# Four attention layers on one core: layer B's state folded into its output weights, PSUM banks handed out singly, loads reordered

## The chip, the cores and the metric

One core of one Trainium2 chip. The metric is the device time of one execution in microseconds; the median of three runs before the change is 563.27 us (559.5 to 564.46).

## The reference

Activations x are 2048 rows of 512 in bf16, 32 heads of 16. Four layers A, B, A, B are each added to x after a layer norm:

```
A: q,k,v = ln(x) @ wqkv;  p = softmax(q k^T / 4) over the keys 0 to 255 rows back;  x + (p v) @ wo
B: pq, pk = phi(q), phi(k)      with phi(t) = (t + 1 if t > 0 else exp(t)) + 1e-6
   kv[h] = sum over rows of pk v^T (16 x 16),   z[h] = sum over rows of pk
   o = (pq kv) / (pq z + 1e-6);   x + o @ wo
```

Both A layers share one set of weights, and both B layers another.

## The kernel before, in words

All of x stays in SBUF in f32 (`xres`, 16 tiles of 128 rows). A superblock I is four tiles, 512 rows; there are four of them. The program is a list of operations, each with a cost per engine, a priority and its dependences; `Planner.run` (L150) is a list scheduler in Python that writes the order of every engine's instructions at build time. At each step it takes the operation that can start first by its own costs, and between equal starts the one with the lower priority number, then the one made first. Operations marked `EV` (priority -1: evacuations) win ties. On the chip the order per engine is fixed and only semaphores decide when an instruction starts.

PSUM has eight banks: a tile of three for one kind of score block (ring "3"), a tile of two for the other (ring "2"), and three single banks (ring "M") for all else: projections, transposes, the p v sums, layer B's products. `Ring.free_at` hands out the buffer that has been free longest.

Layer A, per superblock: `ln_tile` (L399) takes statistics on VectorE, the power on GpSimd and applies them on either; the normalized tile is transposed, by TensorE (`by_pe`) with an evacuation, or by a DMA on SyncE's queue. `prep` (L780) projects k, q and v; k goes into a doubled, masked `kbd` (VectorE, L473), v through `vst` and four DMAs into block-diagonal `vbd` (L492), which is zeroed at the start by GpSimd (L351). `scores` (L497) is matmul, exp on ScalarE (L534) and triangle masks on GpSimd or VectorE; `pv_group` (L571) sums p v and divides; `out_A` (L621) transposes and projects with `woA`.

Layer B, first half (`b_proj`, L787): k and v of four tiles, `phi` (L651: exp on ScalarE, two VectorE operations), the sum into `kvs` (L710), and phi(q) transposed into `pqT` for all 2048 rows. Its work for superblock I is planned between the attention work of later superblocks. When all four are in, `kv_final` (L719) masks the sums into block-diagonal `kvn` and `kvz`. Second half: `den_unit` (L729) multiplies `pqT` by `kvz` for a superblock (16 small matmuls) and takes the reciprocal on VectorE; `p2_tile` (L748) per tile multiplies `pqT` by `kvn` (4 matmuls of 128 columns), multiplies by the reciprocal on VectorE into `ob`, transposes `ob` by TensorE or DMA into `oT`, multiplies by `woB` (4 matmuls of 512 columns), and adds to x, or in the last layer writes `ost` and stores it. For the first B layer these operations are made in the loop of the second A layer, superblock by superblock; for the second they are the last stage.

Loads: x tiles 0 to 3 alternate between SyncE's and ScalarE's queues, wA follows in three pieces on both; woA, wB, woB are three large transfers on SyncE; the other twelve x tiles come by fours on both queues at planned times.

Of the kernel before, what the change touches and what calls it, by code (L numbers as in the profile page):

```python
# [16 lines left out]
P = 128  # L17
# [79 lines left out]
class Ring:  # L97

    def __init__(self, n):
        self.n, self.tiles = n, [None] * n  # L100

    def free_at(self):

        b = [(0.0 if t is None else t.end + .1, k) for k, t in enumerate(self.tiles) if t is None or not t.left]
        return min(b, default=None)


class Slot:
# [13 lines left out]
class Planner:  # L122
# [27 lines left out]
    def run(self, log=None):  # L150
# [9 lines left out]
        ready = {o: max([o.after]) for o in self.ops if not waits[o]}  # L160
# [9 lines left out]
        while ready:  # L170
            best = None
            for o, t in ready.items():
                ok = True
                for s in o.takes:
                    f = s.ring.free_at()
                    if f is None:
                        ok = False
                        break
                    t = max(t, f[0])
                if not ok:  # L180
                    continue
# [10 lines left out]
            for p, t in ready.items():  # L192
                if p is o or e not in p.cost or (p.prio, p.n) >= (o.prio, o.n) or t > start + .02:
                    continue
                if any((s.ring.free_at() or (1e9,))[0] > start + .02 for s in p.takes):
                    continue
# [3 lines left out]
            if e == "PE":  # L200
                if o.kind == "scores" and mode != "scores" or o.kind != "scores" and mode == "scores":
                    start += .05
# [8 lines left out]
            for s in o.takes:  # L211
                s.k = s.ring.free_at()[1]
                s.before = s.ring.tiles[s.k]
                s.ring.tiles[s.k] = s
# [4 lines left out]
            if log is not None:  # L219
                log.append((start, o.end, e, o.kind, o.n, o.prio))  # L220
# [10 lines left out]
def build(ctx, tc, A_x, A_wqkv, A_wo, B_x, B_wqkv, B_wo, out, force_safe=False):  # L231
# [21 lines left out]
    def load_wA():  # L253
        for j in range(3):
            (nc.sync if j % 2 == 0 else nc.scalar).dma_start(
                wA[:, :, j * D:(j + 1) * D], A_wqkv[:, j * D:(j + 1) * D].rearrange("(c p) n -> p c n", p=P))

    def load_rest():
        nc.sync.dma_start(woA[:], A_wo.rearrange("(c p) n -> p c n", p=P))
        nc.sync.dma_start(wB[:], B_wqkv.rearrange("(c p) n -> p c n", p=P))  # L260
        nc.sync.dma_start(woB[:], B_wo.rearrange("(c p) n -> p c n", p=P))

    def load_x(I):
        for u in range(4):
            i = 4 * I + u
            (nc.sync if i % 2 == 0 else nc.scalar).dma_start(x0(i), x_dram[i])

    load_x(0)
    load_wA()

# [13 lines left out]
    nc.vector.tensor_scalar(eo[:, 0:1], eo[:, 1:2], -1.0, 1.0, op0=ALU.mult, op1=ALU.add)  # L284
    ones_bf = consts.tile([P, 1], BF, name="ones_bf")
# [18 lines left out]
    def fast_network(ctx_f):  # L304
        pool = lambda name, bufs, **kw: ctx_f.enter_context(tc.tile_pool(name=name, bufs=bufs, **kw))
        ps3 = pool("ps3", 1, space=PSUM)
        ps2 = pool("ps2", 1, space=PSUM)
        psM = pool("psM", 3, space=PSUM)
# [6 lines left out]
        rings = {"M": Ring(3), "3": Ring(1), "2": Ring(1), "xnT": Ring(3), "xn": Ring(4), "oT": Ring(4), "ost": Ring(3),  # L315
                 "phi": Ring(2), "pks": Ring(3), "vs": Ring(3), "ln": Ring(8), "rden": Ring(2)}
        for k_, r_ in rings.items():
            r_.name = k_
        slot = lambda r: Slot(rings[r])

# [10 lines left out]
        rall = fp.tile([P, NSS, 4, H], F32, name="rall")  # L331
# [3 lines left out]
        kvz = fp.tile([P, NCT, 8], BF, name="kvz")  # L335
# [14 lines left out]
        for k in range(NH):  # L350
            nc.gpsimd.memset(vbd[k][:], 0.0)  # L351
# [10 lines left out]
        def proj(lhs, rhs, prio, reads=(), deps=(), use=(), take=(), pre=None, frees=()):  # L362

            deps = list(deps) + [d for b in frees for d in b.r + b.w]
            s = slot("M")
            t = {}
            def fn(e):
                if pre:
                    pre()
                t["t"] = psM.tile([P, 512], F32, name="ps", tag=f"M{s.k}", bufs=1)  # L370
# [5 lines left out]
        def transpose(src, dst, prio, by_pe, deps, writes=(), use=(), actb=ACTB, take=(), pre=None):  # L376
# [691 lines left out]
```

## Time and profile before

| | us |
|---|---|
| median of three runs | 563.27 |
| the profiled execution's own time | 561.27 |
| its span, first to last instruction | 559.5 |
| TensorE busy | 467.1 (83%) |
| VectorE busy | 385.8 (69%) |
| ScalarE busy | 348.7 (62%) |
| GpSimd busy | 281.4 (50%) |

Busy time is an average over stages. The stages by time: head to 18.5 us, first layer A with the first half of layer B woven in to about 236 us, the end of that first half to 258.5, its second half and the start of the second A layer, that layer to 486, the end of B's first half to 512.7, and B's second half to the end. The granted clock has two levels, 1.2 and 2.4 GHz; a mean between them says how a stretch was shared.

### The profile page before, as it was taken

How to read it: one execution, taken by the hardware profiler on the slowest of the kernel's cores; microseconds unless marked ns; L12 is line 12 of the kernel's file. 1: busy time of each engine (PE TensorE's matmuls, PEld its weight loads, DVE VectorE, ACT ScalarE, POOL GpSimd, SP SyncE). 2: the span in 40 equal slices, each digit the busy share in tenths (PEclk: the TensorE clock that was granted, in tenths of full speed). 3: DMA queues.
4: the chain of work that ended last, by engine and by line, in shares of the span. 5: the costliest groups of instructions: out<-in, count | busy, mean ns of one | idle time of the engine just before them, and what ended most of it. 6: DMA issues, size and time to landing. Idle time of an engine off the chain costs nothing.

```text
span 559.5 us, 14879 instructions
## 1 busy us (share of the span) xinstructions
PE 467.1 (83%) x5828; PEld 240.0 (43%) x5906; DVE 385.8 (69%) x912; ACT 348.7 (62%) x365; POOL 281.4 (50%) x871
## 2 busy tenths in 40 slices
PE   0858979699799999777887979699999999887774
PEld 0324534355445545533433545345555455444332
DVE  2756667477477887657984668687776785969565
ACT  0364838598689999532344759588989899353000
POOL 9343645585385484340752538767767675320000
PEclk9987968899899999798999979999999999998778
DMA  8321313210210120000001023511312120000232
GB/s 274 120 71 47 74 34 69 50 30 21 60 31 12 41 37 2 2 2 1 0 1 41 19 63 61 90 38 27 57 42 40 40 40 2 1 0 3 76 81 75
DMA packets 63789, 24.90 MB, mean 45 GB/s; under 512 B 48352, under 2 KB 63200, under 8 KB 63712
## 3 DMA queue, kind: packets, MB, share of 16 engines
q1 hardware_dynamic: 62032, 22.30, 17.4%
q10 hardware_dynamic: 1680, 1.57, 1.0%
q8 instruction: 48, 0.79, 0.6%
q14 instruction: 29, 0.24, 0.2%
HBM read 6.29 MB, written 2.10 MB: 15 GB/s over the span
## 4 chain that ended last, share of the span: by engine, by line
PE 64%; DVE 14%; DMA 5%; POOL 5%; issue 4%; ACT 3%; SPq 3%; DVEq 0%; ACTq 0%; POOLq 0%
PE ps L372 36%; PE A L516 13%; PE O L587 12%; SPq L492 3%; DMA oT<-ob 3%; ACT pt L534 2%; DVE pqT L660 2%; POOL vbd L351 2%; DVE ln_st L412 2%; DVE xres L454 1%; PE pT L391 1%; DVE rden L744 1%; DVE ob L760 1%; PE pkv L703 1%; DMA vbd<-vst 1%
## 5 line engine op out<-in xcount | busy, mean ns | idle before, releaser
L534 ACT ACTIVATE pt<-A 128x1536 bf16<-128x1536 f32 (+2 forms) x246 | 286.1, 1214 | 71.4 <-PE A L516 39.2
L561 POOL TENSOR_SCALAR_AFFINE_SELECT pt<-pt 128x192 bf16<-128x192 bf16 (+2 forms) x600 | 175.3, 325 | 131.6 <-ACT pt L534 128.6
L516 PE MATMUL A<-qT,kbd 32*128 32x320 bf16 (+4 forms) x1440 | 104.6, 262 | 4.8 <-ACT pt L534 4.4
L587 PE MATMUL O<-vbd,pt 128*128 128x34 bf16 x2880 | 94.8, 180 | 11.1 <-DMA vbd<-vst 10.1
L587 PEld LDWEIGHTS <-pt 128*128 128x128 bf16 x2880 | 83.6, 97 | 35.2 <-issue 19.2
L372 PE MATMUL ps<-xnT,wA 128*128 128x512 bf16 x235 | 68.5, 406 | 14.4 <-ACT pt L534 4.3
L516 PEld LDWEIGHTS <-kbd 32*128 32x128 bf16 x1440 | 38.1, 94 | 78.0 <-issue 71.3
L372 PE MATMUL ps<-wB,xnT 128*128 128x512 bf16 x237 | 63.1, 380 | 2.4 <-DVE o_sb L602 0.4
L556 DVE TENSOR_TENSOR pt<-pt,tri 128x64 bf16<-128x64 bf16 (+4 forms) x217 | 52.3, 267 | 16.2 <-ACT pt L534 15.6
L473 DVE TENSOR_TENSOR kbd<-ps,eo 128x512 bf16<-128x512 f32 x64 | 41.3, 684 | 22.9 <-PE ps L372 20.8
L656 ACT ACTIVATE phi_e<-ps 128x512 bf16<-128x512 f32 x64 | 38.3, 598 | 24.2 <-PE ps L372 22.2
L372 PEld LDWEIGHTS <-xnT 128*128 128x128 bf16 x384 | 31.7, 98 | 40.5 <-issue 11.7
L412 DVE BATCH_NORM_STATS2 ln_st<-xres 128x6 f32<-128x512 f32 (+1 forms) x64 | 43.9, 685 | 7.4 <-DMA xres<-in_A_x_dram 6.9
L416 POOL TENSOR_SCALAR ln_rs<-ln_mv 128x1 f32<-128x1 f32 x64 | 14.5, 227 | 63.6 <-DVE ln_mv L413 61.4
L372 PE MATMUL ps<-woB,oT 128*128 128x512 bf16 x117 | 39.5, 473 | 7.6 <-DMA oT<-ob 4.6
L394 ACT COPY oT<-pT 128x512 bf16<-128x512 bf16 x16 | 9.2, 587 | 58.6 <-PE pT L391 58.6
L372 PEld LDWEIGHTS <-oT 128*128 128x128 bf16 x256 | 24.1, 108 | 45.4 <-issue 18.8
L454 DVE TENSOR_TENSOR xres<-ps,xres 128x512 f32<-128x512 f32 x48 | 32.6, 682 | 13.6 <-PE ps L372 12.7
L372 PEld LDWEIGHTS <-wA 128*128 128x128 bf16 x256 | 22.2, 102 | 42.6 <-issue 24.2
L417 POOL TENSOR_TENSOR ln_rs<-ln_rs,mhalf 128x1 f32<-128x1 f32 x64 | 36.7, 574 | 5.2
L372 PE MATMUL ps<-woA,oT 128*128 128x512 bf16 x118 | 32.4, 393 | 4.5 <-DVE o_sb L602 2.9
L427 POOL TENSOR_SCALAR xn<-xres,ln_mv,ln_rs 128x512 bf16<-128x512 f32 x41 | 32.3, 787 | 5.3 <-DMA oT<-ob 1.1
(72 smaller groups left out, 450.9 us busy)
## 6 DMA issues: line engine op xcount, KB each, us to landing
vbd<-vst SPq DMA_DIRECT2D x128, 34.0 KB, 1.9
out_dram<-ost SPq DMA_DIRECT2D x16, 128.0 KB, 1.7
wB<-in_B_wqkv_dram SPq DMA_DIRECT2D x1, 1536.0 KB, 12.3
xres<-in_A_x_dram SPq DMA_DIRECT2D x8, 128.0 KB, 3.4
xres<-in_A_x_dram ACTq DMA_DIRECT2D x8, 128.0 KB, 2.3
wA<-in_A_wqkv_dram SPq DMA_DIRECT2D x2, 512.0 KB, 9.2
xnT<-xn SPq DMA_TRANSPOSE x44, 2.4
wA<-in_A_wqkv_dram ACTq DMA_DIRECT2D x1, 512.0 KB, 8.6
```

Of the source, the lines that this page charges most:

```text
L372: nc.tensor.matmul(t["t"][:], lhsT=lhs(c), rhs=rhs(c), start=(c == 0), stop=(c == NCT - 1))
L412: nc.vector.bn_stats(t["st"][:], x())
L417: nc.gpsimd.tensor_tensor(t["rs"][:], t["rs"][:], mhalf[:, 0:1], op=ALU.pow)
L427: nc.gpsimd.tensor_scalar(t["xn"][:], x(), t["mv"][:, 2:3], t["rs"][:], op0=ALU.add, op1=ALU.mult)
L454: nc.vector.tensor_tensor(xres[:, i, :], ps()[:], x0(i) if first else xres[:, i, :], op=ALU.add)
L473: nc.vector.tensor_tensor(kbd[r][:, t, :, :, :].rearrange("p m k h -> p (m k) h"), ps()[:, hf * 256:(hf + 1) * 256].unsqueeze(2).to_broadc ...
L516: nc.tensor.matmul(A[:, x, at[x]:at[x] + w, :], lhsT=kbd[half(m)][32 * rg:32 * rg + 32, tt, m % 4, :, :], rhs=qT[I % 2][32 * rg:32 * rg + ...
L534: nc.scalar.activation(body[:, x:y, 0:pos[x], :], t["A"][:, x:y, 0:pos[x], :], ACT.Exp, scale=0.25)
L556: nc.vector.tensor_tensor(v, v, mt, op=ALU.mult)
L561: nc.gpsimd.affine_select(out=v, in_=v, compare_op=ALU.is_ge, fill=0.0, base=1 if kind == 0 else -2, pattern=[[0, n], [2 * sg, 64]], chann ...
L587: nc.tensor.matmul(t["O"][:, u, g, :, :], lhsT=PT[:, s0:s0 + 2, :], rhs=vbd[half(m)][:, m % 4, :, grp[g], :], start=(n == 0), stop=(n == l ...
L656: nc.scalar.activation(t["e"][:], ps()[:], ACT.Exp)
```

## The change

The sums `kvn` are transposed on TensorE and multiplied by `woB` once per layer into `wkv`, so a tile of the second half is four matmuls `pqT` x `wkv` straight into x; `ob`, its transposes and `oT` are gone there. The division moves ahead of it: `norm_unit` broadcasts the denominator over 128 partitions with a masked `zb` (one matmul of 512 columns), takes ln(d + 1e-6) and exp(-...) on ScalarE in place in PSUM, and multiplies `pqT` in place on VectorE. A table set with ln and exp is loaded at the start. All eight PSUM banks are one tensor; `bank()` gives banks 0 to 2 and 3 to 4 to scores and 5 to 7 to the rest, and with `wide` set also 4 and 3. Free buffers go by lowest place, no longer by age. The second VectorE step of phi is split, its first part may go to GpSimd; in some stages k's evacuation may go to ScalarE; `vbd` is zeroed by VectorE. wA comes as k, q, v on SyncE with x 0 to 3 on ScalarE; later x tiles and the other weights come one by one, 128 KB each, on SyncE. Some of the planner's costs change (scores .33 to .23, the four v transfers .4 to 2.45, masks and norms a little up), the check of the softmax sums is made per superblock, and the rings oT and ost have 3 and 2 buffers for 4 and 3.

```diff
-        b = [(0.0 if t is None else t.end + .1, k) for k, t in enumerate(self.tiles) if t is None or not t.left]
+        b = [(max(now, 0.0 if t is None else t.end + .1), k) for k, t in enumerate(self.tiles) if t is None or not t.left]
...
+        def bank(size=1):
+            return Slot(rings["ps"], size, {3: (0,), 2: (3,), 1: (5, 6, 7, 4, 3) if wide[0] else (5, 6, 7)}[size])
...
-    load_x(0)
-    load_wA()
+    for j in (1, 0, 2):
+        nc.sync.dma_start(wA[:, :, j * D:(j + 1) * D], A_wqkv[:, j * D:(j + 1) * D].rearrange("(c p) n -> p c n", p=P))
+    for i in range(4):
+        nc.scalar.dma_start(x0(i), x_dram[i])
+    nc.scalar.preload_act_table_set("natural_log_exp_and_others")
...
-            nc.gpsimd.memset(vbd[k][:], 0.0)
+            nc.vector.memset(vbd[k][:], 0.0)
...
-            pl.op({"SP": .4}, fd, prio, reads=[B("vst", n)], writes=[B("v", half(m0), (m0 % 4) // 2)])
+            pl.op({"SP": 2.45}, fd, prio, reads=[B("vst", n)], writes=[B("v", half(m0), (m0 % 4) // 2)])
...
-                nc.vector.tensor_scalar(t["e"][:], t["e"][:], 1.0, 1e-6, op0=ALU.min, op1=ALU.add)
+                (nc.vector if e == "DVE" else nc.gpsimd).tensor_scalar(t["e"][:], t["e"][:], 1.0, 1e-6, op0=ALU.min, op1=ALU.add)
+            y = pl.op({"DVE": .32, "POOL": (.8, .3)}, f2, EV, deps=[x], use=[es])
...
         def kv_final(prio):
...
+                    nc.vector.tensor_tensor(zb[:, 2 * jj:2 * jj + 2, :], bd[:].unsqueeze(1).to_broadcast([P, 2, P]),
+                                            kvs[jj][:, :, P:P + 1].to_broadcast([P, 2, P]), op=ALU.mult)
...
+            transpose(lambda: kvn[:].rearrange("p t c -> p (t c)"), lambda: kvn[:], prio, True,
+                      [d for jj in range(2) for d in B("kvn", jj).w], writes=[B("kvn", 0), B("kvn", 1)], actb=0.0)
+            for c in range(NCT):
...
+                    nc.tensor.matmul(t["t"][:], lhsT=kvn[:, c, :], rhs=woB[:, c, :], start=True, stop=True)
...
+                evac(lambda c=c: wkv[:, c, :], lambda t=t: t["t"][:], prio, s, deps=[o], writes=[B("wkv", c)], actb=0.0)
...
+        def norm_unit(I, c, prio):
+            s = bank()
             t = {}
+            cols = pqT[:, c, I * 512:(I + 1) * 512]
...
+                nc.tensor.matmul(t["p"][:], lhsT=zb[:, c, :], rhs=cols, start=True, stop=True)
+            o = pl.op({"PE": .22}, f, prio, reads=[B("zb", c // 2), B("pq", I, c)], take=[s], kind="den")
+            def f_r(e):
+                nc.scalar.activation(t["p"][:], t["p"][:], ACT.Ln, bias=eps6[:])
+                nc.scalar.activation(t["p"][:], t["p"][:], ACT.Exp, scale=-1.0)
+            r = pl.op({"ACT": 1.25}, f_r, prio, deps=[o], use=[s])
+            def f_m(e):
+                nc.vector.tensor_tensor(cols, cols, t["p"][:], op=ALU.mult)
+            pl.op({"DVE": .69}, f_m, EV, deps=[r], writes=[B("pq", I, c)], use=[s])
+
+        def p2_tile(i, prio, final=False):
+            out_rows(i, lambda c: pqT[:, c, i * P:(i + 1) * P], lambda c: wkv[:, c, :], prio, [],
+                     reads=[B("pq", i // 4, c) for c in range(NCT)] + [B("wkv", c) for c in range(NCT)], final=final)
...
-        for I in range(1, NI):
-            pl.op({"SP": .2}, lambda e, I=I: load_x(I), 5, writes=b_x[4 * I:4 * I + 4], after=14.0 + 20 * (I - 1))
-        pl.op({"SP": .3}, lambda e: load_rest(), 5, writes=[B("wB"), B("woA"), B("woB")], after=14.0)
+        for i in range(4, NT):
+            pl.op({"SP": .6}, lambda e, i=i: nc.sync.dma_start(x0(i), x_dram[i]), 5, writes=[b_x[i]],
+                  after=(6.0, 24.0, 44.0)[i // 4 - 1] + .7 * (i % 4))
...
+        for c in range(NCT):
+            load(woA, A_wo, B("woA"), c, 16 + 2 * c)
+            for j in range(3):
+                load(wB, B_wqkv, B("wB"), c, 30 + 2 * (4 * j + c), j * D, (j + 1) * D)
+            load(woB, B_wo, B("woB"), c, 70 + 2 * c)
...
         for I in range(NI):
-            R = den_unit(I, 2)
-            for u in range(4):
-                p2_tile(4 * I + u, R, 2, by_pe=True if u % 2 == 0 else False, final=True, actb=0.0)
+            for c in range(NCT):
+                norm_unit(I, c, 2)
+        for i in range(NT):
+            p2_tile(i, 2, final=True)
```

## Rows read from the trace of the kernel before

**Rows 1.** The page: span, engines, granted clock, then the chain of waits by engine.
```profile
span 559.5 us, 14879 instructions
PE 467.1 (83%) x5828; PEld 240.0 (43%) x5906; DVE 385.8 (69%) x912; ACT 348.7 (62%) x365; POOL 281.4 (50%) x871
...
PE 64%; DVE 14%; DMA 5%; POOL 5%; issue 4%; ACT 3%; SPq 3%; DVEq 0%; ACTq 0%; POOLq 0%
```

**Rows 2.** Busy time by stretch, each engine with its instructions; then granted clock, DMA.
```profile
0.00:18.50 18.50, 2.23 (x17) 1.44 (x18) 5.85 (x21) 2.46 (x3) 16.71 (x37) 1.00 0.81 270
36.30:44.70 8.40, 0.48 (x11) 0.36 (x11) 1.13 (x3) 0.64 (x1) 1.53 (x6) 0.67 0.40 99
70.50:74.00 3.50, 0.08 (x4) 0.10 (x1) 1.58 (x4) 0.92 (x1) 0.76 (x3) 0.90 0.05 15
236.00:258.50 22.50, 15.49 (x94) 7.39 (x93) 15.44 (x37) 8.89 (x15) 7.43 (x20) 1.00 0.00 1
258.50:281.70 23.20, 17.93 (x148) 9.75 (x151) 20.15 (x41) 5.21 (x9) 11.50 (x26) 0.85 0.00 1
326.90:363.00 36.10, 27.78 (x395) 14.57 (x399) 24.15 (x59) 23.81 (x22) 24.21 (x75) 0.92 0.39 73
486.00:512.70 26.70, 22.82 (x122) 10.55 (x122) 21.91 (x51) 14.06 (x24) 6.76 (x19) 1.00 0.00 1
512.70:559.50 46.80, 31.33 (x218) 15.59 (x221) 27.82 (x50) 2.34 (x4) 0.00 (x0) 0.76 0.27 70
```

**Rows 3.** Timeline of the head: start, duration, engine, line, operation, idle before.
```profile
3.77 7.47 POOL L351 MEMSET vbd<- 128x2176 bf16 x4
...
13.74 0.23 POOL L416 TENSOR_SCALAR ln_rs<-ln_mv 128x1 f32<-128x1 f32 x1
...
18.50 1.91 PE L372 MATMUL ps<-wA,xnT 128*128 128x512 bf16 x4
```

**Rows 4.** Instructions grouped by line: count, busy us, mean ns, idle before.
```profile
L412 DVE BATCH_NORM_STATS2 ln_st<-xres 128x6 f32<-128x512 f32 (+1 forms) x64 | 43.9, 685 | 7.4 <-DMA xres<-in_A_x_dram 6.9
L349 DVE MEMSET vst<- 128x32 bf16 x2 | 0.2, 85 | 0.1
L286 DVE MEMSET ones_bf<- 128x1 bf16 x1 | 0.1, 59 | 0.0
L394 ACT ACT_TABLE_LOAD x1 | 1.3, 1283 | 2.2 <-issue 2.2
```

**Rows 5.** Timeline of SyncE's queue, the early stretch.
```profile
40.59 5.24 SPq L492 DMA_DIRECT2D vbd<-vst  x8
...
68.33 1.06 SPq L266 DMA_DIRECT2D xres<-in_A_x_dram  x2
```

**Rows 6.** Instructions grouped by line: layer B's second half, and the exponential.
```profile
L756 PE MATMUL pn<-kvn,pqT 128*128 128x128 bf16 x128 | 11.9, 229 | 1.9 <-ACT vst L359 0.8 <-DVE ost L449 0.5 <-DVE ob L760 0.4
L391 PE MATMUL pT<-identb,ob 128*128 128x128 bf16 x64 | 7.8, 259 | 8.6 <-DVE ob L760 8.5
L760 DVE TENSOR_TENSOR ob<-pn,rden 128x512 bf16<-128x512 f32 x32 | 20.6, 684 | 1.8 <-PE pn L756 0.8 <-DVE rden L744 0.2 <-DVE vint L1019 0.2
L744 DVE RECIPROCAL rden<-rden 128x128 f32<-128x128 f32 x8 | 7.6, 953 | 0.2
L656 ACT ACTIVATE phi_e<-ps 128x512 bf16<-128x512 f32 x64 | 38.3, 598 | 24.2 <-PE ps L372 22.2 <-DVE pqT L660 0.8 <-DVE pt L556 0.5
```

**Rows 7.** Timeline from the end of the first layer B.
```profile
258.70 0.49 PE L738 MATMUL pd<-kvz,pqT 128*128 128x8 bf16 x14 [1.31 <-DVE kvz L722]
...
281.69 1.03 PE L372 MATMUL ps<-xnT,wA 128*128 128x512 bf16 x4
```

**Rows 8.** Timeline of the last stage.
```profile
530.39 2.76 PE L372 MATMUL ps<-woB,oT 128*128 128x512 bf16 x12 [0.56 <-DMA oT<-ob]
...
540.12 4.81 PE L372 MATMUL ps<-woB,oT 128*128 128x512 bf16 x12 [0.99 <-DMA oT<-ob]
...
554.29 0.69 DVE L449 TENSOR_TENSOR ost<-ps,xres 128x512 bf16<-128x512 f32 x1 [0.17 <-PE ps L372]
```

More of the change, by code (lines that the diff above doesn't have):

```diff
@@ L159, in run @@
                 users.setdefault(d, []).append(o)
-        ready = {o: max([o.after]) for o in self.ops if not waits[o]}
+        ready = {o: o.after for o in self.ops if not waits[o]}
         mac, warm, mode = {}, {}, ""
@@ L194, in run @@
                     continue
-                if any((s.ring.free_at() or (1e9,))[0] > start + .02 for s in p.takes):
+                if any((s.ring.free_at(s, t) or (1e9,))[0] > start + .02 for s in p.takes):
                     continue
@@ L211, in run @@
             for s in o.takes:
-                s.k = s.ring.free_at()[1]
-                s.before = s.ring.tiles[s.k]
-                s.ring.tiles[s.k] = s
+                s.ring.put(s, s.ring.free_at(s, start)[1])
             for s in o.slots:
@@ L284, in build @@
     nc.vector.tensor_scalar(eo[:, 0:1], eo[:, 1:2], -1.0, 1.0, op0=ALU.mult, op1=ALU.add)
+    eps6 = consts.tile([P, 1], F32, name="eps6")
+    nc.vector.memset(eps6[:], 1e-6)
     ones_bf = consts.tile([P, 1], BF, name="ones_bf")
@@ L330, in fast_network @@
         o_sb = fp.tile([P, 4, D], BF, name="o_sb")
-        rall = fp.tile([P, NSS, 4, H], F32, name="rall")
+        rall = [fp.tile([P, 4, H], F32, name=f"rall{k}") for k in range(2)]
+        okw = fp.tile([P, NSS, 2], F32, name="okw")
+        okt = fp.tile([P, 4 * H], BF, name="okt")
         pqT = fp.tile([P, NCT, S], BF, name="pqT")
@@ L413, in f_bn @@
                 nc.vector.bn_aggr(t["mv"][:, 0:2], t["st"][:])
-            bn = pl.op({"DVE": .85}, f_bn, prio, reads=[B("x", i)], take=[ls])
+            bn = pl.op({"DVE": .9}, f_bn, prio, reads=[B("x", i)], take=[ls])
             def f_rs(e):
@@ L498, in scores @@
             nu = len(units)
-            s = slot(str(size))
+            s = bank(size)
             n = npt[size] % NPT
@@ L523, in scores @@
             reads |= {B("k", half(8 * I + x[0]), p // 4) for (b, p), r in zip(units, runs) for x in r}
[L524 removed]
+            mm = pl.op({"PE": .23}, f_mm, prio, reads=reads, deps=lastmm + list(bPT.r), take=[s], kind="scores")
             lastmm[:] = [mm]
@@ L731, in den_unit @@
+        def norm_unit(I, c, prio):
+            s = bank()
             t = {}
+            cols = pqT[:, c, I * 512:(I + 1) * 512]
             def f(e):
-                t["r"] = small.tile([P, 4, H, 1], F32, name="rden", tag=f"rden{rs.k}", bufs=1)
-                t["p"] = psM.tile([P, 4, H], F32, name="pd", tag=f"M{s.k}", bufs=1)
-                for u in range(4):
-                    for c in range(NCT):
-                        i = 4 * I + u
-                        nc.tensor.matmul(t["p"][:, u, 8 * c:8 * c + 8], lhsT=pqT[:, c, i * P:(i + 1) * P], rhs=kvz[:, c, :],
-                                         start=True, stop=True)
```

204 lines of the change are left out of this document (100 added, 104 removed).

## The prediction

> **What bounds the kernel now.** I read the page first: TensorE is busy 83% of 559.5 us and carries 64% of the chain of waits, VectorE 14% [rows 1]. That is an average, so I took stretches next [rows 2]. In the long attention stretches TensorE has the least slack. The idle time lies at seams: the head (2.23 us of TensorE work in 18.5), a hole from 36.3 to 44.7 us (0.48 of 8.4), another from 70.5 to 74.0, the passage between layers from 258.5 to 281.7, where VectorE is busy 20.15 of 23.2 us, the stretch from 326.9 to 363 (27.78 of 36.1), and the last stage, 46.8 us with TensorE busy 31.33 at a mean granted clock of 0.76, a mixture of the 1.2 and 2.4 GHz levels [rows 2]. The timelines then say what each seam waits for [rows 3, 5, 7, 8]. The change touches all of them.
>
> **The head.** GpSimd zeroes vbd until 11.2 us and so reaches the first layer norm's power only at 13.74; the first projection starts at 18.50 [rows 3]. VectorE had its four statistics long before. The change hands the zeroing to VectorE. No row shows a long memset there. The two short ones give 85 ns for 32 elements and 59 for one, 0.84 ns per element, so 2176 elements take 1.9 us and five 9.4, from 1.3 to 10.7 us [rows 4]. The first statistic (0.69 and a small aggregate [rows 4]) is then done at about 11.6, and the first power can follow there instead of at 13.74; from there on the chain to the first projections is as long as now (4.8 us [rows 3]). So some 2 us are gained. Bounds: 0 if an element costs a full nanosecond and more, 9 if the memsets cost next to nothing and the statistics run at 4 us as now. I take 2, from the nearest rows.
>
> The Trainium skill (VectorE: DVE Perf Modes, Zero memsets can be issued as uint32 (trn2)) says that a memset costs one cycle per element whatever the type, and that a VectorE memset of zero can go out as uint32 words, at half the elements. By it the five would take about 4.7 us, and the sum below would be 4.7 us lower, 526; GpSimd's row of 2176 bf16 elements shows no such form, and no run here shows it on VectorE.
>
> **The two early holes.** From 36.3 to 44.7 us p v waits for the vbd transfers. A group of four takes SyncE 2.6 us to issue (eight in 5.24 [rows 5]), while the plan charges 0.4, so the order puts transposes ahead of groups that p v needs. Charged 2.45, the plan can see this. Four groups are 10 us of queue whatever the order, and they can start only behind the v projections; I take 5 of the 8.4 us, bounds 0 and 8. From 70.5 to 74.0 VectorE, and TensorE behind it, waits for x tiles whose transfer was issued at 68.33, behind a group of vbd [rows 2, 5]; singly and planned from 44 us on they are in time: 3.4, bounds 0 and 3.4.
>
> Against this, 20 weight pieces and 12 x tiles now go through SyncE, at 0.53 us each (two in 1.06 [rows 5]) 17 us of issue, less six x issues that were there already: 14. What is queued behind one of them (a vbd group, a transposing DMA) is late by 0.53. They have the lowest priority; I charge 2 us, bounds 0 and 8.
>
> **Between the layers, per layer B.** Removed per tile: 4 matmuls on kvn (11.9 us for 128 [rows 6]: 0.37), the multiply into ob (0.684), a transpose on TensorE with its evacuation or a DMA; per superblock 16 small matmuls (14 in 0.49 [rows 7]) and the reciprocal (0.953 [rows 6]). Added per superblock: four wide matmuls (0.23 each, from 12 in 2.76 [rows 8]), eight ScalarE passes, four multiplies. No row shows ln or an in-place PSUM pass; exp of the same size from PSUM takes 0.598 [rows 6], so a unit is 1.2 us of ScalarE; half and double would be 0.6 and 2.4. The multiply I price at 0.69 as the one into ob, which also reads a bank. Folding adds two VectorE masks, a transpose and four matmuls with evacuations, about 3.8 us from the last sum, in the shadow of the first four units (0.5 + 4 x 1.2 + 0.7 = 6.0 us). If that shadow were missing it would cost 3.8.
>
> From 258.5, superblock 0's first add to x would then end at about 7.6 us (0.92 and 0.69 later) and the fourth at 12.5. A statistic and the 4.8 us of the head's chain later, at 18, k and q could start, instead of at 23.2 (281.69 [rows 7]). But all 16 units may start at once and have priority 1.5, ahead of the norms' and projections' 2 and 2.2. VectorE, today the busiest here, sheds 8 x 0.684 + 2 x 0.953 = 7.4 us and gets up to 16 x 0.69 = 11. So the gain lies between 5 and nothing; I take 3.
>
> **Inside the second A layer** superblocks 2 and 3 leave TensorE 8 x 0.37 + 2 x 0.56 = 4.1 us of work, and eight DMA transposes go. Of the 8.3 us that TensorE is idle between 326.9 and 363 [rows 2] I count a third, 2.9. Together 7; bounds 3 and 12.
>
> **Ends of layer B's first half** (236 to 258.5, 486 to 512.7): two more banks, and GpSimd, busy 7 us in each [rows 2], may take phi's short step. Today's chain there runs through layer norm, which stays. I take 2 in both together, bounds 0 and 6.
>
> **The last stage.** ScalarE gets 16 x 1.2 = 19.1 us where it now has 2.34 [rows 2]; VectorE 32 x 0.69 = 22; TensorE 16 tiles at 0.92 us each at the upper clock or 1.60 at the lower (12 matmuls in 2.76 and in 4.81 [rows 8]). The 32 matmuls that transpose ob, with their waits (8.5 us behind ob in the kernel [rows 6]), and the four blocks of reciprocal, multiply, transpose and project, 46.8 us in all, go. They don't shrink to 22, because of the order: units and tiles have one priority and the units are made first, so as long as a unit is left, every free bank goes to it. With five banks the sixteenth unit's matmul waits for the eleventh's multiply, at 0.5 + 11 x 1.2 + 0.7 = 14.4 us. TensorE is nearly idle until then, and I expect the first tiles at the lower clock: three by 19.5, three more by 24.3, ten at 0.92 by 33.5. From the last output's start to the end it is 5.2 us today (554.29 to 559.5 [rows 1, 8]). 39 us against 46.8: 8. Two more where the masks slip in before the last phi is done, as now GpSimd may take part of phi: 10. Bounds: 4 (no overlap, all tiles slow) and 17 (bound by VectorE alone).
>
> **Sum.** 2 + 5 + 3.4 - 2 + 3 + 7 + 2 + 10 = 30.4. The profiled execution's own time is 561.27, 1.8 above its span and 2.0 below the median of 563.27, inside the runs' spread of 5; so 531 us.
>
> **Rivals.**
> Deeper: the memsets run at half my price, the units overlap the last q projections, so that the last stage comes near its VectorE bound. For it: ScalarE and GpSimd idle there; against: the order just told. 531 - 4.7 - 7 - 8 (the rest of the second layer's 12 and of the passage) = 511.
>
> Given back in attention: free banks now go by lowest place instead of longest free, and the changed costs reorder all of it. Projections and p v sums, some 270 in the program, share three banks. Where the real release lags the planned one, the wait falls on TensorE, which has little slack; at 0.1 us each this is 27 us, at half of that 14. For it: the plan's times already miss by microseconds at 36 and 70 us; against: three banks that are nearly always taken leave little choice. 545 to 558, middle 551.
>
> Slower: ln and exp evict each other's table. The row shows one load of 1.283 us in the whole kernel, for copy and exp [rows 4]. If each unit loaded twice, it would cost 2.57 us more on ScalarE: in the last stage 16 units on the path, 41 us; in the passage 4 to 16 units, 10 to 41. It decides from 24 exposed loads (31 us) on, and gives 582 to 613. Against it: the program names one set with both at its start. The Trainium skill (ScalarE: Activation LUTs, Table sets: the hidden batching unit) puts ln and exp into that one set, which would make the loads none; no run here has used ln yet.
>
> It does not do what it says: if the one PSUM tensor were guarded as a whole and not by bank, scores and projections would take turns and nothing would overlap; 700 us or more. It can't be seen in the profile of before.
>
> **How the numbers follow.** Forecast with its own range of 515 to 546: 0.62. Deeper, 496 to 515: 0.15. Given back, 545 to 565: 0.15. Tables: 0.06. One tensor: 0.02. A change of this kernel can be told from none at 1%, 557.6 to 568.9. Faster: 0.62 + 0.15 + two thirds of 0.15 = 0.87. Same: 0.05. Slower: 0.08. Leaving out the lower half of the deeper case (0.07) and the upper part of the others (0.13) gives 506 to 549.
>
> **What would show it.** The memset's duration on VectorE and the first projection's start (16.4 us, or 11.7 with short memsets). No hole longer than 4 us at 36 to 45 and at 70. 64 ScalarE passes of 0.6 us for the units and a single table load. k and q of the second A layer 20 us after the first layer B's last sum. No transposing DMA between 326 and 363. In the last stage outputs that begin only some 14 us after the masks, at the lower clock at first. I am wrong if TensorE's busy share in the attention stretches falls, which would be the banks, or if the last stage is not bound by its order.

## The result and the profile after

The changed kernel takes 535.66 us in the median of four runs (533.38 to 539.18), the kernel before 563.59 beside it: a ratio of 0.952 [0.945, 0.960]. The forecast was 531. The profiled execution of the changed kernel is its slowest, 539.18, with a span of 537.5; between the two profiles lie 22.0 us, between the medians 27.9. The accounts below are made in spans.

The page of the changed kernel, the lines that answer to [rows 1]:

```profile
span 537.5 us, 14479 instructions
PE 464.3 (86%) x5634; PEld 228.1 (42%) x5634; DVE 386.7 (72%) x902; ACT 383.8 (71%) x432; POOL 301.0 (56%) x885
...
PE 50%; POOL 14%; DVE 12%; ACT 10%; DMA 6%; issue 4%; SPq 2%; DVEq 0%; POOLq 0%; ACTq 0%
```

The change took little from TensorE (467.1 to 464.3), put 35 us on ScalarE and 20 on GpSimd, and GpSimd's share of the chain rose from 5% to 14%. That last number is the first to ask about.

Busy time by stage, columns as in [rows 2]. The bounds are the same events in both kernels: the first projection, the last p v sum of superblock 0 and of superblock 3, the end of the second mask, the second A layer's first k projection, then the last sums of superblocks 0 and 2, the second mask again. The kernel before:

```profile
18.50:83.37 64.87, 51.07 (x564) 24.40 (x570) 40.88 (x95) 35.33 (x37) 27.65 (x91) 0.84 0.23 57
83.37:232.35 148.98, 136.61 (x2003) 71.43 (x2025) 102.98 (x270) 124.35 (x122) 88.54 (x286) 0.94 0.16 33
232.35:258.50 26.15, 18.78 (x113) 9.24 (x114) 18.95 (x45) 9.96 (x17) 7.43 (x20) 0.97 0.01 2
258.50:281.69 23.19, 17.92 (x147) 9.75 (x150) 20.15 (x41) 5.21 (x9) 11.50 (x26) 0.85 0.00 1
281.69:339.22 57.53, 49.47 (x614) 25.00 (x621) 36.38 (x72) 33.16 (x33) 25.94 (x89) 0.91 0.14 33
339.22:435.56 96.34, 89.56 (x1362) 46.48 (x1374) 71.41 (x175) 81.10 (x75) 69.31 (x214) 1.00 0.27 50
435.56:513.18 77.62, 70.41 (x823) 36.90 (x834) 61.82 (x155) 54.84 (x67) 34.34 (x110) 1.00 0.09 15
513.18:559.50 46.32, 31.05 (x213) 15.32 (x213) 27.34 (x48) 2.34 (x4) 0.00 (x0) 0.76 0.28 71
```

The changed kernel, the same stages with the head in front, and the two holes of [rows 2] at the end:

```profile
0.00:17.42 17.42, 1.44 (x13) 1.18 (x14) 14.28 (x26) 2.05 (x3) 7.64 (x32) 1.00 0.48 151
17.42:68.61 51.19, 47.47 (x579) 23.07 (x578) 39.24 (x88) 37.69 (x44) 28.28 (x92) 1.00 0.41 104
68.61:214.28 145.67, 137.87 (x2021) 70.84 (x2020) 103.48 (x269) 124.33 (x122) 102.07 (x303) 0.94 0.20 39
214.28:240.46 26.18, 20.25 (x118) 9.77 (x118) 19.74 (x49) 10.11 (x18) 9.42 (x21) 0.95 0.00 1
240.46:266.06 25.60, 20.29 (x75) 7.99 (x75) 21.62 (x42) 19.89 (x37) 8.11 (x19) 0.73 0.00 1
266.06:322.12 56.06, 52.18 (x601) 24.65 (x601) 39.62 (x85) 37.13 (x42) 31.39 (x99) 0.94 0.18 36
322.12:412.87 90.75, 88.37 (x1350) 46.64 (x1347) 68.26 (x170) 80.08 (x76) 65.18 (x206) 1.00 0.21 41
412.87:494.99 82.12, 70.53 (x804) 35.24 (x803) 57.86 (x146) 54.25 (x66) 48.90 (x117) 0.93 0.07 14
494.99:537.50 42.51, 25.86 (x84) 8.75 (x82) 22.62 (x36) 18.29 (x33) 0.00 (x0) 0.74 0.16 51
36.30:44.70 8.40, 7.99 (x124) 4.18 (x123) 7.74 (x19) 5.22 (x7) 4.44 (x14) 1.00 0.54 147
70.50:74.00 3.50, 3.50 (x30) 1.29 (x31) 3.24 (x9) 3.12 (x4) 3.16 (x12) 1.00 0.71 70
```

Read the second column down both. One bound is not the same event: in the kernel before, 258.50 is the start of the second mask, which ends at 258.98; the two terms beside it are counted from there. Gained: head 1.1 (18.50 to 17.42), first superblock 13.7, the next three 3.3, the end of B's first half 0.4, the passage minus 2.9, then 1.5, 5.6 and minus 4.5 in the second A layer, last stage 3.8: 22.0 in all. Both holes are full of TensorE work. The forecast total is near, its composition is not.

One profile doesn't fix every term. The kernel with four output buffers by lowest place (below) issues the changed kernel's instructions in the same order, and its own profile has 53.24 us for 56.06 in superblock 0 of the second A layer, 79.71 for 82.12 in the stage behind superblock 2, and 44.89 for 42.51 in the last stage; the other six stages agree within 0.6. So terms of these three stages are uncertain by 2 to 3 us.

Groups by line of the changed kernel, which answer to [rows 4, 6]:

```profile
L690 DVE SCALAR_TENSOR_TENSOR pks<-psb,phi_e 128x512 bf16<-128x512 f32 x32 | 22.0, 688 | 10.0 <-POOL phi_e L687 9.3
L690 DVE SCALAR_TENSOR_TENSOR pqT<-psb,phi_e 128x512 bf16<-128x512 f32 x32 | 21.9, 687 | 13.9 <-POOL phi_e L687 13.5
L687 POOL TENSOR_SCALAR phi_e<-phi_e 128x512 bf16<-128x512 bf16 x15 | 29.2, 1947 | 13.1 <-ACT phi_e L684 7.5 <-DVE kvs L740 4.9
L687 DVE TENSOR_SCALAR phi_e<-phi_e 128x512 bf16<-128x512 bf16 x49 | 15.5, 316 | 8.9 <-ACT phi_e L684 8.4
L782 ACT ACTIVATE psb<-psb,eps 128x512 f32<-128x512 f32 x32 | 21.2, 663 | 9.1 <-PE psb L779 9.1
L783 ACT ACTIVATE psb<-psb 128x512 f32<-128x512 f32 x32 | 18.6, 582 | 1.0
L470 DVE TENSOR_TENSOR ost<-psb,xres 128x512 bf16<-128x512 f32 x16 | 10.5, 689 | 9.2 <-DMA out_dram<-ost 9.1
L366 DVE MEMSET vbd<- 128x2176 bf16 x5 | 9.4, 1872 | 2.0 <-issue 2.0
L275 ACT ACT_TABLE_LOAD x1 | 1.3, 1283 | 2.7 <-issue 2.7
```

Phi's short step takes 1947 ns on GpSimd, where the plan charges 0.8 us, and 316 on VectorE; VectorE waits 9.3 + 13.5 = 22.8 us for it. A norm unit costs ScalarE 0.663 + 0.582 = 1.245 us. The outputs wait 9.1 us for stores: behind the third they come in pairs, one pair in 2.54 us.

```profile
516.72 1.29 DVE L470 TENSOR_TENSOR ost<-psb,xres 128x512 bf16<-128x512 f32 x2 [1.35 <-DMA out_dram<-ost]
519.25 1.29 DVE L470 TENSOR_TENSOR ost<-psb,xres 128x512 bf16<-128x512 f32 x2 [1.24 <-DMA out_dram<-ost]
```

### The profile page after: what moved, and what is told of

Read it like the earlier page. It is cut to its first block, busy times and chain, and to the rows that moved or that the text cites. A ratio compares the mean times of both kernels' runs of the same rounds, so it can differ in the third digit from the quotient of the medians.

```text
span 537.5 us, 14479 instructions
## 1 busy us (share of the span) xinstructions
PE 464.3 (86%) x5634; PEld 228.1 (42%) x5634; DVE 386.7 (72%) x902; ACT 383.8 (71%) x432; POOL 301.0 (56%) x885
## 4 chain that ended last, share of the span: by engine, by line
PE 50%; POOL 14%; DVE 12%; ACT 10%; DMA 6%; issue 4%; SPq 2%; DVEq 0%; POOLq 0%; ACTq 0%
PE psb L387 28%; PE psb L540 10%; PE psb L611 10%; POOL phi_e L687 5%; POOL pt L585 4%; ACT pt L558 4%; ACT psb L782 3%; ACT psb L783 3%; DMA out_dram<-ost 2%; DVE ln_st L427 2%; POOL xn L442 2%; SPq L516 2%; DVE vbd L366 2%; POOL ln_rs L432 2%; DMA oT<-o_sb 1%
## 5 line engine op out<-in xcount | busy, mean ns | idle before, releaser
L558 ACT ACTIVATE pt<-psb 128x1536 bf16<-128x1536 f32 (+2 forms) x246 | 286.0, 1216 | 49.6 <-PE psb L540 36.6
L540 PE MATMUL psb<-qT,kbd 32*128 32x320 bf16 (+4 forms) x1440 | 103.0, 260 | 2.9 <-ACT pt L558 2.8
L611 PE MATMUL psb<-vbd,pt 128*128 128x34 bf16 x2880 | 94.0, 179 | 5.7 <-DVE pqT L690 1.4
L387 PE MATMUL psb<-xnT,wA 128*128 128x512 bf16 x256 | 65.8, 384 | 6.5 <-DVE xn L439 3.0
L387 PE MATMUL psb<-wB,xnT 128*128 128x512 bf16 x256 | 68.7, 401 | 2.2 <-ACT xnT L409 0.7
L580 DVE TENSOR_TENSOR pt<-pt,tri 128x192 bf16<-128x192 bf16 (+4 forms) x206 | 54.9, 294 | 16.2 <-ACT pt L558 15.7
L684 ACT ACTIVATE phi_e<-psb 128x512 bf16<-128x512 f32 x64 | 38.4, 601 | 20.6 <-PE psb L387 10.0
L497 DVE TENSOR_TENSOR kbd<-psb,eo 128x512 bf16<-128x512 f32 x57 | 36.9, 682 | 11.3 <-PE psb L387 11.2
L387 PE MATMUL psb<-wkv,pqT 128*128 128x512 bf16 x128 | 34.6, 420 | 4.4 <-DVE ost L470 2.9
L687 POOL TENSOR_SCALAR phi_e<-phi_e 128x512 bf16<-128x512 bf16 x15 | 29.2, 1947 | 13.1 <-ACT phi_e L684 7.5
L387 PE MATMUL psb<-wA,xnT 128*128 128x512 bf16 x128 | 34.6, 401 | 1.8 <-DMA xnT<-xn 1.8
L387 PEld LDWEIGHTS <-wA 128*128 128x128 bf16 x256 | 21.2, 98 | 32.6 <-issue 13.5
```

The source lines that it names most:

```text
L387: nc.tensor.matmul(t["t"][:], lhsT=lhs(c), rhs=rhs(c), start=(c == 0), stop=(c == NCT - 1))
L497: nc.vector.tensor_tensor(kbd[r][:, t, :, :, :].rearrange("p m k h -> p (m k) h"), ps()[:, hf * 256:(hf + 1) * 256].unsqueeze(2).to_broadc ...
L540: nc.tensor.matmul(A[:, x, at[x]:at[x] + w, :], lhsT=kbd[half(m)][32 * rg:32 * rg + 32, tt, m % 4, :, :], rhs=qT[I % 2][32 * rg:32 * rg + ...
L558: nc.scalar.activation(body[:, x:y, 0:pos[x], :], t["A"][:, x:y, 0:pos[x], :], ACT.Exp, scale=0.25)
L580: nc.vector.tensor_tensor(v, v, mt, op=ALU.mult)
L611: nc.tensor.matmul(t["O"][:, u, g, :, :], lhsT=PT[:, s0:s0 + 2, :], rhs=vbd[half(m)][:, m % 4, :, grp[g], :], start=(n == 0), stop=(n == l ...
```

## The experiments

**What the loads and v's price do alone.** The kernel before with

```diff
-            pl.op({"SP": .4}, fd, prio, reads=[B("vst", n)], ...
+            pl.op({"SP": 2.45}, fd, prio, reads=[B("vst", n)], ...
```

> The kernel before with one number changed: the plan charges a group of four v transfers 2.45 us instead of 0.4. The prediction's term: the hole from 36 to 45 us loses 5 us, nothing else moves, 558. First rival (the plan's whole order is nearer to the chip, so every superblock of both A layers gains): 545 to 552, with the end of the first superblock's attention 8 us or more earlier and later superblocks shorter too. Second rival (the order shuffles and nothing is gained): 561 to 566.

Measured: 527.76 us, ratio 0.937 [0.930, 0.943], better than the whole change and below all three expectations. The two holes of [rows 2] in this kernel:

```profile
36.30:44.70 8.40, 5.38 (x16) 1.88 (x16) 2.68 (x4) 0.17 (x1) 1.06 (x5) 0.50 0.44 103
70.50:74.00 3.50, 3.34 (x76) 2.47 (x75) 3.15 (x9) 3.09 (x3) 2.49 (x10) 1.00 0.14 33
```

The first transfers are no earlier (the first two groups are issued at 21.2 and 31.0 us, at 21.2 and 31.5 before). What is new is TensorE's order: the plan now knows that vbd is late and puts projections (5.38 us) where p v stood and waited (0.48). The superblocks' attention ends at 75.45, 121.57, 165.38 and 213.21 us, where it ended at 83.37, 136.07, 184.71 and 232.35: the first three superblocks are 7.9, 6.6 and 4.8 us shorter, the fourth and superblocks 1 to 3 of the second A layer (140.3 us, 140.9 here) are not. VectorE's wait of 4.05 us for x at 70 us is gone too, though the loads are the old ones; behind the head the longest left is 1.56. From the second A layer's last p v sum to the end it took 80.0 us (from 479.47) and takes 66.5 (from 458.19). Of these 13.5 us, 6.1 lie ahead of the last mask, where 4 steps of phi(q) are left instead of 16, and 7.4 in the last stage, whose code is the old one:

```profile
458.19:485.76 27.57, 21.35 (x120) 9.94 (x121) 19.81 (x49) 9.37 (x16) 7.50 (x20) 0.87 0.01 2
485.76:524.70 38.94, 26.80 (x217) 15.18 (x218) 25.82 (x42) 4.09 (x7) 0.00 (x0) 0.85 0.34 83
```

So the old last stage, at a mean granted clock of 0.85 instead of 0.76 and with shorter waits for `ob`, is 3.6 us shorter than the changed one (42.51). One number in the plan reordered the program far beyond the operation that it prices.

The same with all of the change's loads (x and weights one by one on SyncE, wA as k, q, v):

> The kernel before with that number and with all of the change's loads: wA as k, q, v on SyncE, x 0 to 3 on ScalarE's queue, later x tiles and 20 weight pieces one by one on SyncE. vbd is still zeroed by GpSimd. The prediction's terms: 5 + 3.4 - 2, so 557. Rival from the trace of after (its first two superblocks end 14.8 and 20.4 us earlier than before, more than the terms of the head and the two holes): the loads and the v price carry nearly all of the gain in the first A layer, 545 to 548, with the second superblock's attention ending at about 118 instead of 136 us.

523.96, ratio 0.931 [0.924, 0.937]: some 4 us less than with the price alone, but the two intervals overlap, so a worth of the loads themselves isn't shown.

The folding alone (`zb`, `wkv`, `norm_unit`, the short `p2_tile`) in the kernel before, with its banks, prices and loads:

> The kernel before with the folding alone: zb, wkv, the units with ln and exp, tiles as four matmuls; old banks (three single ones by age), old loads, old prices; the per-superblock check of sums and three oT buffers come along, because SBUF is full otherwise. By the prediction's terms for passage, second A layer and last stage (3 + 7 + 10): 543. Rival from the trace of after, where the second A layer with its passage is as long as before and the last stage some 3 us shorter: 557 to 562. With three output buffers instead of two the last stage may be 4 us better than in after.

557.27, ratio 0.991 [0.987, 0.995]: 6 us, the rival. From the last p v sum to the end it saves 15 (80.0 to 65.0), but between the last p v sum of one A layer and the first superblock's of the next it loses 7.2 (106.9 to 114.1), and 10.1 in the three superblocks after that (140.3 to 150.4). The first A layer, where none of the folded work runs, ends 6.7 us earlier (225.67 for 232.35), so by the plan's new order and what came along with the edit; without these the rest is 2.3 us longer. The last stage, counted from the second `zb`, takes 39.0 us, the 39 of the prediction: with three output buffers by longest free the outputs come one in 0.86 us and hardly wait for stores.

```profile
L461 DVE TENSOR_TENSOR ost<-ps,xres 128x512 bf16<-128x512 f32 x16 | 11.1, 691 | 3.4 <-PE ps L378 3.0 <-DMA out_dram<-ost 0.3
```

The changed kernel with v's old price:

> The changed kernel with the planner's price of v's four transfers put back from 2.45 to 0.4; nothing else. Alone on the kernel before, that price brought 35 us. Theory: it is the same lever here, the plan again believes in p v sums whose transfers are still on the queue, and VectorE's and TensorE's idle time behind vbd comes back in the first and the second A layer: 560 to 571. Rival: the change's new order of loads and its other prices already spread the queue, so the lever is worth less than 10 us here: 538 to 545.

556.13, ratio 0.992 [0.988, 0.996]: 20 us worse by the medians and 16.9 by the spans, 10.7 of these by the end of the first superblock. The rival, under 10, falls, and the theory's 560 to 571 is missed by 4. The price is worth 35 without the other parts and 20 with them.

**Phi's step on GpSimd.** The changed kernel with

```diff
-            y = pl.op({"DVE": .32, "POOL": (.8, .3)}, f2, EV, ...
+            y = pl.op({"DVE": .32}, f2, EV, ...
```

> The kernel after, with phi's short step on VectorE only. In after GpSimd does 15 of the 64 at 1.95 us each (the plan charges 0.8) where VectorE takes 0.29, VectorE waits 22.8 us for them in all, and they are 5.3% of the chain. If those waits are on the path: 518 to 527. If the waits are covered by other work or come back as VectorE's own load (15 x 0.3 = 4.5 us): 534 to 537. If GpSimd's share saves VectorE where it is the bound: 538 and more.

522.46, ratio 0.925 [0.920, 0.931]: the step on GpSimd costs 13 us of the change's gain, 10.7 of the 17.0 between the spans in superblocks 1 to 3 of the second A layer (147.6 to 136.9); 5.1 and 6.2 come in the stretches ahead of them, and 5.0 are lost again behind the last p v sum. The plan orders other work anew as well, so the 13 hold a share of reordering that wasn't told apart. Its groups by line, 64 steps on VectorE and the wait gone:

```profile
L690 DVE SCALAR_TENSOR_TENSOR pks<-psb,phi_e 128x512 bf16<-128x512 f32 x32 | 22.0, 688 | 0.8
L690 DVE SCALAR_TENSOR_TENSOR pqT<-psb,phi_e 128x512 bf16<-128x512 f32 x32 | 21.9, 686 | 0.5
L687 DVE TENSOR_SCALAR phi_e<-phi_e 128x512 bf16<-128x512 bf16 x64 | 19.8, 309 | 10.6 <-ACT phi_e L684 9.4
```

This kernel differs from the one with price and loads (523.96, the same chip) by folding, banks, memset, the smaller rings and the other prices. All these together are worth 1.5 us, within the intervals.

**The banks.** The changed kernel without banks 4 and 3 for single use:

```diff
-            return Slot(..., 1: (5, 6, 7, 4, 3) if wide[0] else (5, 6, 7)}[size])
+            return Slot(..., 1: (5, 6, 7)}[size])
```

> The changed kernel without the two additional single banks: projections, sums and norm units keep banks 5, 6 and 7 in all stages, as many as before. Theory of the prediction (two more banks are worth 2 us at the two ends of layer B's first half, and let the units of the last stage run ahead): three banks still hold a unit each, whose round of matmul, two passes and multiply is some 3.2 us, so ScalarE's 1.24 us stays the pace; 2 to 4 us lost, 538 to 540. Rival 1: the banks are most of what the change brings outside the loads; then over 8 us are lost, 544 and more. Rival 2: nothing or a gain, 530 to 536, since fewer units run ahead of the tiles.

555.62, ratio 0.989 [0.984, 0.995]: 20 us lost, 10.6 of the 17.4 between the spans from one A layer's last p v sum to the first superblock's of the next (107.8 to 118.4), 10.2 behind the second layer's last p v sum (67.8 to 78.0), and 3.7 given back between. The theory's 2 to 4 falls, the first rival holds. Its timeline at the end of B's first half (start, duration, engine, line, operation, wait before it):

```profile
226.27 1.95 POOL L687 TENSOR_SCALAR phi_e<-phi_e 128x512 bf16<-128x512 bf16 x1
228.25 0.69 DVE L690 SCALAR_TENSOR_TENSOR pks<-psb,phi_e 128x512 bf16<-128x512 f32 x1 [2.96 <-POOL phi_e L687]
229.00 3.57 PE L387 MATMUL psb<-wB,xnT 128*128 128x512 bf16 x8 [2.42 <-DVE pks L690]
```

The projection waits for the bank that the GpSimd step keeps: with phi there, a bank is held for 0.6 + 1.95 + 0.69 us. So a part of these 20 us is what the additional banks hide of the 13. It can't be all: by the stages of the tables 5.8 are lost at this end, but 10.0 in the passage and 9.8 in the last stage (and 5.2 and 4.5 come back in superblock 0 of the second A layer and behind superblock 2), and in neither of those two does a step of phi start on GpSimd. In the last stage the first three units' matmuls start 3.1 us apart (501.04, 504.21, 507.33; 493.24, 493.47, 493.76 with five banks), the second behind the last phi step, the third behind the products for `wkv`. From there on ScalarE sets the pace, a unit in 1.18 us, as the theory had it (1.24), but the first output comes 24.0 us behind the mask instead of 17.8. How the 20 divide wasn't tried.

**The last stage.** Four kernels; its length is counted from the second `zb` (494.24 in the changed kernel, 43.3 us to the end). First more output buffers, `"ost": Ring(4)` for `Ring(2)`:

> The changed kernel with four buffers for the output tiles (ost) instead of two; only the last stage uses them. Theory: behind its last norm unit the last stage is paced by the stores. In the changed kernel six pairs of outputs follow each other every 2.54 us while TensorE needs 1.89 us a pair, and VectorE waits 9.1 us in all for stores. With four buffers TensorE sets the pace: 6 x 0.65 = 4 us less, 531.5, and the wait of the output addition on a store all but goes. Rival: the queue that issues the stores or the stores themselves set the pace whatever the buffers (2.5 us a pair stays), 535.7 and the wait only moves to the end.

539.48, ratio 0.960 [0.953, 0.967]; every engine has the changed kernel's order of instructions, and the pairs of outputs still follow every 2.54 us. The lowest free buffer is taken, and the plan believes a store over after 0.6 us, so the third buffer, it seems, is never reached. Two kernels that issue the same instructions in the same order thus differ by 3.8 us when timed apart; smaller differences of such medians say nothing. With four buffers by longest free:

```diff
+class Oldest(Ring):
+    def free_at(self, slot, now):
+        b = min([(0.0 if t is None else t.end + .1, k) for k, t in ...], default=None)
+        return b and (max(now, b[0]), b[1])
...
-        rings = {... "ost": Ring(2), ...
+        rings = {... "ost": Oldest(4), ...
```

> The changed kernel with four output buffers (the four of the normalized tiles, idle in the last stage) that are handed out by longest free, the rule of the kernel before, in place of two by lowest place; order of work elsewhere unchanged. With four buffers by lowest place the pairs of outputs kept their 2.54 us: the plan prices a store at 0.6 us, believes the lowest buffer free by then, and never reaches the third. Theory: with the old rule all four are used, VectorE's wait for stores (9.1 us in the changed kernel) falls under 3 us and the last twelve outputs run at TensorE's 0.95 us each: 0.3 x 13 = 4 us less, 531.5. Rival: one queue issues and lands a store in 1.27 us whatever the buffers, the pace stays at 2.54 us a pair, 535.7.

528.87, ratio 0.938 [0.930, 0.946]; the stage takes 36.2 us. The outputs, written to the four tiles of the normalized rows, which are idle by then, wait no more for stores:

```profile
513.77 2.50 DVE L478 TENSOR_TENSOR xn<-psb,xres 128x512 bf16<-128x512 f32 x4 [1.01 <-PE psb L395]
516.44 0.69 DVE L478 TENSOR_TENSOR xn<-psb,xres 128x512 bf16<-128x512 f32 x1 [0.17 <-PE psb L395]
517.30 0.69 DVE L478 TENSOR_TENSOR xn<-psb,xres 128x512 bf16<-128x512 f32 x1 [0.17 <-PE psb L395]
```

One output in 0.86 us, by TensorE's pace, for one in 1.27. Then the order, each superblock's tiles behind its units:

```diff
-                norm_unit(I, c, 2)
-        for i in range(NT):
-            p2_tile(i, 2, final=True)
+                norm_unit(I, c, 2 + .1 * I)
+            for u in range(4):
+                p2_tile(4 * I + u, 2.05 + .1 * I, final=True)
```

> The changed kernel with one difference in the last stage's order: the four tiles of a superblock come right behind the norm units of that superblock, ahead of the next superblock's units; amount of work unchanged. Theory of the prediction (the stage is bound by its order, units before tiles): the first output starts some 6 to 8 us behind the first unit instead of 18 (494.2 to 512.0 in the changed kernel), the tiles hide under ScalarE's 16 x 1.24 = 19.8 us, and only the last four tiles and the stores (4 x 1.3 + 5.3) stand behind the last unit: 494.2 + 20 + 1 + 10.5 = 526, against 537.5; the run at 524 to 527. Rival: the tiles take banks and VectorE from the units, whose rate falls from one in 1.2 us to one in 1.8 and more, so that the end moves by less than 3 us: 533 to 536.

533.34, ratio 0.946 [0.939, 0.954]; the stage takes 42.0, only 1.3 less, which is inside what the stage varies by between profiles: the rival. The first output comes 10.8 us behind the second mask instead of 17.8, but the tiles then hold the banks while they wait for two store buffers, and no unit's matmul starts from 497 to 509 us (columns as in the timeline above):

```profile
505.85 1.29 DVE L470 TENSOR_TENSOR ost<-psb,xres 128x512 bf16<-128x512 f32 x2 [2.17 <-DMA out_dram<-ost]
...
508.40 1.29 DVE L470 TENSOR_TENSOR ost<-psb,xres 128x512 bf16<-128x512 f32 x2 [1.25 <-DMA out_dram<-ost]
509.14 0.38 PE L779 MATMUL psb<-pqT,zb 128*128 128x512 bf16 x1 [0.66 <-DVE ost L470]
```

**The memset.** `vbd` allocated as f32 words and zeroed as such, the same bytes:

```diff
-            nc.vector.memset(vbd[k][:], 0.0)
+            nc.vector.memset(vbd_w[k][:], 0.0)
```

> The changed kernel with vbd's five zeroing memsets written as f32 words, half the elements, the same bytes, still on VectorE; plan and orders unchanged. Theory by the number of elements: 1088 elements at 0.86 ns are 0.95 us each instead of 1.87, so the first power and the first projection start 4.6 us earlier (12.8 instead of 17.4) and the run is 4 to 4.7 us shorter, 531. Rival 1, by bytes: 1.87 each, nothing changes, 535.7. Rival 2: the memsets are shorter, but the first statistic then waits for x (4 us from the store in memory) or the first projection for its weights, and under 2 us come out: 534.

533.11, ratio 0.947 [0.940, 0.954]. The duration goes by elements, and the first projection starts at 11.78 us instead of 17.42:

```profile
L367 DVE MEMSET vbd<- 128x1088 f32 x5 | 4.8, 965 | 0.9 <-issue 0.9
```

The first superblock ends 5.4 us earlier and the span is 5.0 shorter; the medians show 2.5, less than they can tell.

**Together.** Phi on VectorE, f32 memset, tiles behind their units, four buffers by longest free:

> The changed kernel with four edits together: phi's short step on VectorE alone (13 us alone), vbd zeroed as f32 words (5.1 us in the profile, 2.5 in the medians), in the last stage each superblock's tiles right behind its units (2.3 to 5.9 us alone, held up by waits of 8.8 us for the two output buffers), and four output buffers handed out by longest free. Theory: they touch different stretches and add: 522.5 - 4 - 8 = 510, with the first output 8 us behind the first unit, and no wait for stores over 3 us. Rival: the edits overlap, as with one wait gone the last stage becomes bound by VectorE's 32 passes of 0.69 us plus the low clock of its start: 515 to 519.

506.76 us, ratio 0.905 [0.900, 0.911], faster than both kernels and than each edit alone. The last stage takes 32.3 us: buffers alone brought 7.1, order alone 1.3, both 11. Its page:

```profile
span 504.9 us, 14406 instructions
PE 450.0 (89%) x5560; PEld 226.5 (45%) x5634; DVE 383.6 (76%) x907; ACT 383.4 (76%) x431; POOL 277.7 (55%) x878
```

Last, to this kernel, `norm_unit(I, c, 1.5 if I == 0 else 2.5)` between the layers:

> The kernel of the four edits together (506.8) with one priority changed: between the layers the norm units of superblocks 1 to 3 get 2.5 in place of 1.5, behind superblock 0's norms and projections; the units of superblock 0 stay ahead. Theory: the passage from the masks to the second A layer's first k evacuation (225.6 to 258.8 there, 33.2 us; 26.5 in the kernel before) is long because all 16 units, 16 x 1.24 us on ScalarE and 16 x 0.69 on VectorE, are made ahead of superblock 0's norms. With 4 units there it is 25 to 28 us, and the other 12 fit beside attention: 500. Rival: ScalarE is the tight engine of attention (90% busy in the best stretches), so the 12 x 1.24 = 15 us come back in the second A layer's first two superblocks: 504 to 510, with a short passage and longer superblocks.

511.5, ratio 0.909 [0.905, 0.913], above both expectations; from the first mask to the first k evacuation 32.7 us (33.2 without the edit), and superblocks 1 and 2 of the second A layer are 5.8 us longer. The matmuls of all 16 units still ran by 246 us: the plan takes what can start first, a priority only breaks ties, and ScalarE was free. The edit didn't do what it should, so where the units belong stays open.

## Why the prediction was right, point by point

**The head: price right, gain half, and not where forecast.** 1872 ns against 1.9 forecast, 1.1 us gained against 2. The sum left out the gaps, 0.40 us ahead of each long memset, 2.0 in all. So the first statistic starts at 12.62 us and the first power at 13.61, not at 11.6, hardly before the 13.74 of the kernel before; the 1.1 us come from the chain behind it, 3.8 us instead of 4.8.

```profile
8.03 0.10 DVE L286 TENSOR_SCALAR par_i<-pidx 128x1 int32<-128x1 int32 x1
8.54 1.87 DVE L366 MEMSET vbd<- 128x2176 bf16 x1 [0.40 <-issue]
12.62 0.69 DVE L427 BATCH_NORM_STATS2 ln_st<-xres 128x6 f32<-128x512 bf16 x1
13.61 0.23 POOL L431 TENSOR_SCALAR ln_rs<-ln_mv 128x1 f32<-128x1 f32 x1 [8.41 <-DVE ln_mv L428]
```

One reading was off: VectorE had only three of the four statistics "long before"; in the kernel before the fourth stands at 15.37 us, behind the first power. The f32 kernel shows 0.965 us for half the elements. The Trainium skill (VectorE: DVE Perf Modes, Zero memsets can be issued as uint32 (trn2)) has a memset cost by element whatever the type, and these two rows agree; the smaller form didn't come by itself, it had to be written.

**The early holes and the loads: 6.4 forecast (5 + 3.4 - 2), 17.0 measured** in the first A layer. The step that failed is "four groups are 10 us of queue whatever the order; I take 5 of the 8.4". I priced the transfers' wait, when what counted was what TensorE does meanwhile, and I priced one hole, when the wrong number stood behind the order of three superblocks and of the last stage. The 3.4 for single x loads came with the price alone too. The price alone gave 35 us. That is the mechanism of the first-named danger, "the changed costs reorder all of it", with the sign turned.

**The passage: 3 forecast, -2.9 measured.** Its bound, "between 5 and nothing", failed. All 16 units did run ahead of k and q, as feared: ScalarE is busy 19.9 of 25.6 us (5.2 of 23.2 before), TensorE's mean granted clock is 0.73 (0.85), and k and q come 25.6 us behind the masks, not 20.

**The second A layer: 7 forecast, 2.6 measured** (1.5 + 5.6 - 4.5; 7.7 in the other profile of the same order). A third of 8.3 is 2.8, not 2.9; the 7 stands. The work did go (of the transposes in that stretch those of `ob`; the A layer's own stay, so "no transposing DMA" was said too widely), but no run shows it to be worth 7: the folding alone makes these three stages 1.8 us longer in sum. The GpSimd step, which the prediction mentioned only as a help ("may take phi's short step"), cost more in the same stretches: without it they are 14.5 us shorter than in the kernel before. This is the mis-sized term with the opposite sign: I never priced that step on GpSimd, and no row of before showed it. The trace of after shows 1947 ns against 316, six times. The Trainium skill (GPSIMD Engine Reference, Engine selection) advises VectorE for elementwise work and calls GpSimd's one-input operations roughly line-rate; the advice agrees with the run without GpSimd, the rate doesn't with these rows.

**The ends of B's first half: 2 forecast for both; 0.4 in the first**, and the second lies in the stage that lost 4.5. The two more banks were taken for a small help; they carry 20 us, most of them in the passage and the last stage; the sum counts with five banks in the last stage and gives them no price there.

**The last stage: 10 forecast, 3.8 measured** (1.4 in the other profile). The order was as foretold: units first, one in 1.2 us, the first output 17.8 us behind the mask and the third 20.4 (three by 19.5 forecast), the first tiles at the lower clock (a granted clock of 0.50, which is 1.2 GHz, from 509.5 to 512.5 us). The step that failed is "ten at 0.92": they came in pairs every 2.54 us behind two store buffers. A change named in the text, the ring of 2 for 3 and the lowest place, had no price in the sum; with four buffers by longest free, and with the three of the folding alone, the tiles run at 0.86, and the latter's stage has the 39 us of the sum.

**The rivals.** One table load of 1283 ns and no further: tables out. The one PSUM tensor isn't guarded as a whole: 700 us or more didn't come. Given back in attention: something was, 13 us, and the run without GpSimd's step has it back with the banks still by lowest place. What the old rule for the banks would give wasn't run, but the sign named for it didn't show: TensorE's busy share rose in four of the five stretches of attention (79 to 93%, 92 to 95, 86 to 93, 93 to 97) and fell only behind superblock 2 (91 to 86), where GpSimd has eight of its 15 steps. Deeper (511) names a place that only the four edits reached, 506.8.

So the total came out within 5 us because two errors met, and that is luck: the plan's price was worth far more than I charged, and four side effects that I charged at nothing or as a gain (GpSimd, units in the passage, store buffers, memset gaps) took it back. Of the sum's mechanisms the order of the last stage came as told, and the rest with other sizes or for other reasons.

## What to carry to other kernels

In a program whose order is written by a planner, compare each price in it with the trace before costing any removed work: 0.4 for 2.45 us of queue, 0.8 for 1.95 us of GpSimd and 0.6 for a store that lands later went with 20 to 35, 13 and 7 us, folding with 6. Only the first was set right as a price; for the others the work was taken off GpSimd and the buffers were handed out by another rule. A change of many parts is read by running its parts alone; their worths don't add (35 alone, 20 within). A rule that hands out the lowest free buffer makes more buffers useless if the plan frees them too early.

## What the runs showed of the hardware

- The same one-input step on 128x512 bf16 takes 1947 ns on GpSimd and 316 on VectorE.
- Ahead of each of five VectorE memsets of 1.87 us there is a gap of 0.38 to 0.40 us, ahead of each of five of 0.96 us one of 0.15 to 0.18, and no wait is shown for either.
- In place on a PSUM bank in f32, ln with a bias takes 663 ns and exp 582.
